# Attention into a gated MLP on one core: weight transfers a piece ahead, moves four a step, the low halves split later, output and spatial groups alternating

## The chip, the core and the metric

The kernel runs on one core of a Trainium2 chip. The metric is device microseconds of that core, lower is better: the median of three runs before the change is 774.14 us (772.09 to 775.22).

## The reference

Eight batches of 576 positions. Attention with 8 heads of 64, masked by blocks of 64 positions, is followed by a gated MLP whose gate mixes positions (`w_spatial`). All is float32.

```python
scores = q @ k.T / sqrt(64)                  # per batch and head, 576 x 576, block-causal mask
attn   = exp(scores - max) / (sum + 1e-9)
x      = attn @ v                            # heads side by side: 576 x 512 per batch
h      = max(x @ w_in, 0)                    # 512 -> 1024
u, v   = h[..., :512], h[..., 512:]
v_n    = (v - mean(v)) / sqrt(var(v) + 1e-6)
v_s    = einsum('ts,bsd->btd', w_spatial, v_n) + b_spatial
out    = (u * v_s) @ w_out                   # 512 -> 512
```

## The kernel before

The work is laid out by hand in **steps**, counted by `n`. Heads go in pairs, four pairs a batch, 32 pairs in all, and a pair takes `NS = 7` steps (`i` is the step within the pair, `g` the pair). In each step the program text issues, in a fixed order, a few instructions for each engine. `own` keeps every compute instruction in program order on its engine, so an instruction that waits holds back all that stands behind it on that engine. A step is an order and not a time: an engine runs on into later steps as far as its waits let it.

One pair passes through these stations:

- `load_pair` (SP, step 0 of the pair before): queries and keys into `raw`. `prep_pair`: ScalarE rounds them to `hi`, GpSimd subtracts for `lo` in four pieces (lines 237 to 251). Batch 0 uses `raw` directly, later batches three products of `hi` and `lo`.
- `scores_last` and `scores` (TensorE, steps 0 and 3; in batch 0 also 1 and 5): the last 64 queries of both heads first, then two banks at a time. `scores_last` needs the **last** of the four `lo` pieces in its third matmul.
- `exps` (VectorE maximum, ScalarE exponential; one slot a step), `norm` (VectorE reciprocal, GpSimd scaling, in the step after the slots 0, 2, 4 and 6).
- turning the probabilities: in batch 0 and for the last pair TensorE does it (`transposes_pe`, two steps after the slot) and ScalarE copies the result out at once, in batch 0 into the one tile `turned`. All other pairs turn 32x32 blocks on VectorE (`transposes`, three steps after), into a tile `q`, and `move` puts the quarters in place in `turned` with 16 transfers, all issued in step 3 of the next pair.
- `av` (TensorE): attention times values, at step `AV_AT = 17` after the pair's start, `BOOT_AV = 9` in batch 0, `LAST_AV = 10` for the last pair. ScalarE and VectorE split the result into the two halves of `x`.

When a batch's last `av` is out, `begin` puts the MLP's 29 **groups** of matmuls in `queue`: five `v_group`, eight `u_group`, and for each half `z` of the positions four `sp_group` (the spatial product, followed by gate and split into `gh` and `gl`) and four `out_group`. A credit counter lets them out at about one a step, at the end of the step, after the attention work. Each group's follow-up work is hung on later steps with `later(steps, phase, f)`: phase 0 opens a step, phase 1 follows exps, transposes and norm, phase 2 closes it.

The weights come in pieces (eight of `w_in`, four and a tail of `w_spatial`, four of `w_out`). `prep_w` issues one transfer into a staging buffer (the buffers of `gh` and `gl`, one each), four VectorE operations, one ScalarE copy and one GpSimd subtraction; `spread` hands these out over given steps as background work, emitted behind phase 1.

```python
        due(1)
        step_background(n)
        if at(n - 2) and by_pe(at(n - 2)[:2]):
            for j in TURNS[(i - 2) % NS]:
                transposes_pe(*at(n - 2)[:2], j)
        credit = min(credit + rate, 2.0)
        while credit >= 1.0 and queue and queue[0][0]():
            queue.pop(0)[1]()
            credit -= 1.0
```

## Time and profile before

| | before |
|---|---|
| median of 3 runs | 774.14 us |
| profiled run: time, span | 776.13 us, 774.3 us |
| granted TensorE clock, mean | 0.947 |
| busy: TensorE / VectorE / ScalarE / GpSimd | 695.3 / 468.5 / 430.8 / 341.5 us |
| first scores of batch 1 (step 28) | at 70.19 us |
| first MLP group of batch 0, of batch 1 | at 80.50, 204.76 us |
| first MLP group of the last batch | at 716.34 us |

Busy time says how long an engine had an instruction in work. TensorE is the engine with the most of it, so the first thing to look for is where TensorE sat idle, or ran at a lower granted clock, and what it waited for there.

### The profile page before, as it was taken

How to read it: one execution, taken by the hardware profiler on the slowest of the kernel's cores; microseconds unless marked ns; L12 is line 12 of the kernel's file. 1: busy time of each engine (PE TensorE's matmuls, PEld its weight loads, DVE VectorE, ACT ScalarE, POOL GpSimd, SP SyncE). 2: the span in 40 equal slices, each digit the busy share in tenths (PEclk: the TensorE clock that was granted, in tenths of full speed). 3: DMA queues.
4: the chain of work that ended last, by engine and by line, in shares of the span. 5: the costliest groups of instructions: out<-in, count | busy, mean ns of one | idle time of the engine just before them, and what ended most of it. 6: DMA issues, size and time to landing. Idle time of an engine off the chain costs nothing.

```text
span 774.3 us, 16381 instructions
## 1 busy us (share of the span) xinstructions
PE 695.3 (90%) x5729; PEld 611.9 (79%) x5729; DVE 468.5 (61%) x1587; ACT 430.8 (56%) x1156; POOL 341.5 (44%) x525
## 2 busy tenths in 40 slices
PE   6885943979998999899998999899998999899998
PEld 4554732968887988798887988798897988789897
DVE  5766837847666667665576666766676567521430
ACT  5665754545565547655575556755655556542542
POOL 3546644645433653355432663265435544231011
PEclk9797975999999999999998999999999999899999
DMA  6332253256554555546553565556553655140001
GB/s 212 105 105 93 81 141 115 67 127 174 156 125 96 148 150 149 133 114 157 147 133 76 144 156 132 133 152 162 149 121 89 174 154 122 39 124 25 15 13 49
DMA packets 42150, 92.05 MB, mean 119 GB/s; under 512 B 9298, under 2 KB 18002, under 8 KB 42068
## 3 DMA queue, kind: packets, MB, share of 16 engines
q1 hardware_dynamic: 32852, 81.56, 41.0%
q10 hardware_dynamic: 9216, 9.44, 3.5%
q8 instruction: 45, 0.74, 0.4%
q14 instruction: 37, 0.30, 0.1%
HBM read 38.18 MB, written 9.44 MB: 61 GB/s over the span
## 4 chain that ended last, share of the span: by engine, by line
PE 57%; DVE 15%; DMA 8%; ACT 6%; POOL 5%; SPq 5%; issue 4%; POOLq 0%; ACTq 0%; DVEq 0%
PE mv L514 10%; PE mo L667 10%; PE ms L632 9%; PE avh L466 6%; PE mu L608 5%; PE s L284 5%; SPq L420 4%; PE avl L466 3%; DMA turned<-q 3%; DVE q L405 3%; PE avh L483 2%; DVE p L319 2%; POOL p L353 2%; DMA raw<-qk 2%; PE s L296 1%
## 5 line engine op out<-in xcount | busy, mean ns | idle before, releaser
L353 POOL TENSOR_SCALAR p<-p,ssum 128x384 f32<-128x384 f32 (+4 forms) x288 | 162.7, 579 | 253.3 <-DVE ssum L349 135.3
L335 ACT ACTIVATE p<-p,nmax 128x384 f32<-128x384 f32 (+4 forms) x288 | 167.1, 581 | 110.8 <-DVE nmax L319 68.9
L319 DVE CUSTOM_DVE_ANT_0 p<-s,mask 128x128 f32<-128x128 f32 (+3 forms) x256 | 117.9, 480 | 26.7 <-PE s L284 26.5
L405 DVE STREAM_TRANSPOSE q<-p 128x384 f32<-128x384 f32 (+1 forms) x189 | 110.1, 615 | 9.7 <-DMA turned<-q 8.8
L608 PE MATMUL mu<-x,wi_hi 128*128 128x288 f32 x512 | 114.9, 306 | 0.0
L248 POOL TENSOR_TENSOR lo<-raw,hi 128x288 fp32r<-128x288 f32 x112 | 92.1, 848 | 1.0 <-ACT hi L244 1.0
L608 PEld LDWEIGHTS mu<-x,wi_hi 128*128 128x128 f32 x512 | 88.1, 196 | 3.1 <-issue 0.4
L651 POOL TENSOR_TENSOR gl<-u,gh 128x288 fp32r<-128x288 f32 x64 | 51.1, 806 | 88.4 <-ACT gh L650 88.4
L641 DVE TENSOR_TENSOR u<-ms,u 128x288 f32<-128x288 f32 x64 | 29.1, 454 | 92.7 <-PE ms L637 92.7
L514 PE MATMUL mv<-wi_hi,x 128*128 128x512 f32 x256 | 85.1, 395 | 0.0
L667 PE MATMUL mo<-gl,wo_hi 128*128 128x288 f32 x256 | 77.5, 303 | 3.8 <-POOL gl L651 3.3
L667 PE MATMUL mo<-gh,wo_hi 128*128 128x288 f32 x256 | 78.1, 305 | 0.0
L632 PE MATMUL ms<-ws_hi,vh 128*128 128x288 f32 x256 | 77.1, 301 | 0.3 <-DVE x L441 0.3
L667 PE MATMUL mo<-gh,wo_lo 128*128 128x288 f32 x256 | 75.5, 295 | 0.0
L632 PE MATMUL ms<-ws_hi,vl 128*128 128x288 f32 x256 | 75.4, 294 | 0.0
L632 PE MATMUL ms<-ws_lo,vh 128*128 128x288 f32 x256 | 75.3, 294 | 0.0
L608 PE MATMUL mu<-x,wi_lo 128*128 128x288 f32 x256 | 72.4, 304 | 0.0
L284 PE MATMUL s<-hi 64*128 64x128 f32 (+1 forms) x224 | 48.8, 388 | 17.1 <-DVE nmax L319 16.9
L466 PE MATMUL avh<-turned,v 128*64 128x128 f32 x868 | 57.0, 286 | 0.0
L514 PEld LDWEIGHTS mv<-wi_hi,x 128*128 128x128 f32 x256 | 48.1, 188 | 10.9 <-PE s L284 0.4
L667 PEld LDWEIGHTS mo<-gl,wo_hi 128*128 128x128 f32 x256 | 48.1, 188 | 8.1 <-POOL gl L651 7.5
L544 DVE BATCH_NORM_STATS2 st<-vr 128x6 f32<-128x512 f32 (+1 forms) x40 | 27.5, 689 | 44.4 <-ACT vr L532 44.0
(120 smaller groups left out, 1561.5 us busy)
## 6 DMA issues: line engine op xcount, KB each, us to landing
turned<-q SPq DMA_DIRECT2D x216, 100.0 KB, 3.5
turned<-q SPq DMA_DIRECT2D x216, 96.0 KB, 2.2
raw<-qk SPq DMA_DIRECT2D x31, 608.0 KB, 4.6
v<-v SPq DMA_DIRECT2D x32, 320.0 KB, 3.2
outT<-o ACTq DMA_DIRECT2D x64, 144.0 KB, 2.4
rwi<-w_in SPq DMA_DIRECT2D x8, 512.0 KB, 3.9
rwo<-w_out SPq DMA_DIRECT2D x4, 512.0 KB, 3.7
rws<-w_spT SPq DMA_DIRECT2D x4, 288.0 KB, 2.9
```

Source lines behind the costliest of these rows:

```text
L248: own(nc.gpsimd.tensor_tensor(out=lo[:, cs], in0=raw[:, cs], in1=hi[:, cs].bitcast(F32), op=ALU.subtract))
L284: own(nc.tensor.matmul(banks[(b, pr, i + hd)][:, o:o + n], a[js, qs], k[js, :n], start=(m == 0), stop=(m == len(parts) - 1),))
L319: own(nc.vector.tensor_tensor_reduce(out=pt[:, o:o + n], in0=bk[:, o:o + n], in1=mask[:, 512 - n:], scale=-0.125, scalar=BIG, op0=ALU.add, ...
L335: own(nc.scalar.activation(pt[:, o:o + n], pt[:, o:o + n], AF.Exp, bias=mx, scale=-1.0, accum_out=ssum[:, s0 + r:s0 + r + 1],))
L353: own(nc.gpsimd.tensor_scalar(out=pt[:, o:o + w], in0=pt[:, o:o + w], scalar1=ssum[:, r:r + 1], scalar2=1.0, op0=ALU.mult, op1=ALU.mult,))
L405: own(nc.vector.transpose(to[:, :, o:o + 32 * n].rearrange("p r (c j) -> p c r j", j=32), pt[:, :n * P].rearrange("p (c r j) -> p c r j", ...
L466: own(nc.tensor.matmul(out[js, (t0 - q0) * P:(t1 + 1 - q0) * P].rearrange("p (t a j) -> p a t j", a=4, j=32), vt[:, c, js], src[:, :, o:o ...
L514: own(nc.tensor.matmul(ps, xs[k][:, j, cs], w[:, k, DH:], start=(n == 0), stop=(n == 3 * NC - 1),))
L608: own(nc.tensor.matmul(ps[:, :HT], w[:, k, ds], xs[k][:, j, zs], start=(n == 0), stop=(n == 3 * NC - 1),))
L632: own(nc.tensor.matmul(ps[:, :HT], a[:, ds], w[:, k, zs], start=(n == 0), stop=False))
L651: own(nc.gpsimd.tensor_tensor(out=gl[:, dc, :], in0=uz, in1=gh[:, dc, :].bitcast(F32), op=ALU.subtract))
L667: own(nc.tensor.matmul(ps[:, :HT], w[:, k, es], a[:, k, :], start=(n == 0), stop=(n == 3 * ND - 1),))
```

## The change

- **Weights**: two staging buffers for each of the two tags; one generator, `ahead`, issues the transfer of the next piece before the work on the present one; the pieces are spread over other steps (1 to 53 instead of 2 to 45).
- **Moves**: `move` issues four transfers in each of the steps 3 to 6 instead of 16 in step 3.
- **Batch 0 and the last pair**: the turned probabilities get a `q` tile of their own (with its memset), the transposes come four steps after the slot instead of two, the copy out one step later still, and `av` at step 12 (before 9, and 10 for the last pair). `begin` of batch 0 comes at step 34 (before 30). The loads of the values move to later steps.
- **Splitting queries and keys**: `hi` and `lo` have one buffer instead of two. `prep_pair` runs in steps 4 and 5 of the pair before (two `lo` pieces in each) instead of 2 to 4.
- **Order in a step**: in steps 0 and 3 `exps` comes behind the transposes and `norm`. The last part of the normalisation of `v` moves to phase 2.
- **Groups**: the order starts `vv`; the output groups of half 0 alternate with the spatial groups of half 1; `gh` and `gl` have two buffers; the gate of the last spatial group of a half waits for the next step like the others.

```diff
-AV_AT, BOOT_AV, LAST_AV = 2 * NS + RUN2, NS + 2, NS + RUN2
+AV_AT, BOOT_AV = 2 * NS + RUN2, NS + 5
-    hl_p = ctx.enter_context(tc.tile_pool(name="hl_p", bufs=2))
+    hl_p = ctx.enter_context(tc.tile_pool(name="hl_p", bufs=1))
-        t = ff_p.tile([P, ND, HT], F32R, tag=tag, name=f"r{name}")
+        t = ff_p.tile([P, ND, HT], F32R, tag=tag, name=f"r{name}", bufs=2)
...
             own(nc.scalar.copy(hi[:, cs], raw[:, cs]))
         yield
-        yield
         for cs in (slice(S, S + HT), slice(0, HT), slice(HT, S), slice(S + HT, KQ)):
...
-        if (b, pr) == last and i == 0:
-            quarters[last] = tr_p.tile([P, 4, TW], F32, tag="q", name="q_last")
-            nc.gpsimd.memset(quarters[last][64:P, :, Q8O + P:], 0.0)
-        to = quarters.get((b, pr), turned)
+        if i == 0:
+            quarters[(b, pr)] = tr_p.tile([P, 4, TW], F32, tag="q", name=f"q_{b}_{pr}")
+            own(nc.gpsimd.memset(quarters[(b, pr)][64:P, :, Q8O + P:], 0.0))
+        to = quarters[(b, pr)]
...
+        later(1, 0, evac)
...
-    def move(b, pr):
+    def move(b, pr, a):
...
-            for a in range(4):
-                nc.sync.dma_start(turned[32 * r:32 * r + 32, a, :w], t[32 * a:32 * a + 32, r, :w])
+            nc.sync.dma_start(turned[32 * r:32 * r + 32, a, :w], t[32 * a:32 * a + 32, r, :w])
...
-            later(3, 1, rest)
+            later(3, 2, rest)
...
-            later(0 if dc == ND - 1 else 1, 2 if dc == ND - 1 else 0, gate)
-            later(0 if dc == ND - 1 else 1, 2 if dc == ND - 1 else 1, split_g)
+            later(1, 0, gate)
+            later(1, 1, split_g)
...
-        order = "vuvuvuvuvuuuu" if b else "v" * 5 + "u" * 8
+        order = "vvuvuvuvuuuuu" if b else "v" * 5 + "u" * 8
...
-        for z in range(2):
-            queue += sps[z] + outs[z]
-        return queue
+        queue += sps[0] + sps[1][:1]
+        for dc in range(1, ND):
+            queue += [outs[0][dc - 1], sps[1][dc]]
+        return queue + outs[0][ND - 1:] + outs[1]
...
+    def ahead(gens):
+        for k, g in enumerate(gens):
+            if k == 0:
+                next(g)
+            if k + 1 < len(gens):
+                next(gens[k + 1])
+            yield from g
...
+    spread(weights, 6 * NC, 1, U0 - 2)
+    spread(weights, 6 * NC, U0 - 2, U0 + 10)
+    spread(weights, 2 * FULL + 3, U0 + 10, U0 + 17)
+    spread(weights, 6 * ND, U0 + 17, U0 + 25)
+    spread(weights, None, U0 + 25, 0)
...
-            if i == 2 and b > 0:
-                spread(prep_pair(b, pr), 8, n, n + 4)
+            if i == RUN2 + 1 and b > 0:
+                spread(prep_pair(b, pr), 6, n, n + 2)
...
-                    later(1 if b else 0, 3, lambda b=b: begin(b))
-        if at(n - NS - RUN2) and i == RUN2 and not by_pe(at(n - NS - RUN2)[:2]):
-            move(*at(n - NS - RUN2)[:2])
-        if here:
+                    later(1, 3, lambda b=b: begin(b))
+        if g > 0 and RUN2 <= i < RUN2 + 4 and at(n - NS) and not by_pe(pairs[g - 1]):
+            move(*pairs[g - 1], i - RUN2)
+        runs = here and not boot and i in (0, RUN2)
+        if here and not runs:
             exps(*here, i)
...
+        if runs:
+            exps(*here, i)
...
-        if at(n - 2) and by_pe(at(n - 2)[:2]):
-            for j in TURNS[(i - 2) % NS]:
-                transposes_pe(*at(n - 2)[:2], j)
+        if at(n - 4) and by_pe(at(n - 4)[:2]):
+            for j in TURNS[(i - 4) % NS]:
+                transposes_pe(*at(n - 4)[:2], j)
```

## The prediction

> **What bounds the kernel now.** I read the page's busy line and slices first, then busy time by stage, then what TensorE waited for in each stage, and last the neighbours of the longest waits.

> ```profile
> PE 695.3 (90%) x5729; PEld 611.9 (79%) x5729; DVE 468.5 (61%) x1587; ACT 430.8 (56%) x1156; POOL 341.5 (44%) x525
> PE   6885943979998999899998999899998999899998
> PEclk9797975999999999999998999999999999899999
> 0.00:70.19 70.19, 51.51 (x352) 33.01 (x353) 46.33 (x147) 42.10 (x116) 35.31 (x57) 0.85 0.41 132
> 70.19:204.76 134.57, 100.51 (x831) 88.77 (x830) 84.51 (x277) 69.83 (x187) 71.09 (x98) 0.86 0.43 118
> 204.76:716.34 511.58, 489.06 (x4192) 439.25 (x4191) 321.18 (x1118) 296.42 (x804) 228.72 (x364) 0.98 0.50 128
> 462.98:546.32 83.34, 80.36 (x707) 72.28 (x706) 56.43 (x197) 50.84 (x140) 40.02 (x64) 1.00 0.54 139
> ```

> The stage rows give start and end, length, busy time of TensorE, its weight loads, VectorE, ScalarE and GpSimd, then the granted clock. TensorE bounds the kernel from 204.76 us on (489.06 of 511.58 us busy, clock 0.98). Before that it is idle for 204.76 - 51.51 - 100.51 = 52.7 us, at a clock of 0.85. So there are two questions: how much of the first 205 us comes back, and whether the dense part stays dense. Its last row is one batch's period (29 groups and 28 steps of attention) at full clock: 83.3 us.

> The largest hole is one wait of 19 us:

> ```profile
> 126.95 0.61 PE L296 MATMUL s<-hi,lo 128*128 128x288 f32 x1 [19.22 <-POOL lo L248]
> POOL ws_b L197 <- ACT ws_a L194: 7.1, 1, 7.1
> ACT ws_a L194 <- DMA rwt<-w_spT: 8.1, 1, 8.1
> DVE fwo L149 <- DMA rwo<-w_out: 14.2, 2, 11.1
> 100.68 10.13 SPq L420 DMA_DIRECT2D turned<-q  x16
> 110.85 0.59 SPq L190 DMA_DIRECT2D rwt<-w_spT  x1
> 112.35 11.48 SPq L141 DMA_DIRECT2D rwo<-w_out  x3
> SPq L257 <- PE avh L483: 28.0, 4, 9.7
> 126.95:139.50 12.55, 9.92 (x50) 9.23 (x51) 10.71 (x32) 4.87 (x15) 5.97 (x7) 0.58 0.32 96
> ```

> TensorE waits for `lo`; on GpSimd the rest of `lo` stands behind a weight subtraction, that waits for ScalarE, ScalarE for a weight transfer, and that one was queued on SP behind 16 moves that took 10.13 us. VectorE waited 11.1 us for the next piece. SP itself was held four times, 28.0 us, by a load of values that waited for `av`. After the hole TensorE ran 12.55 us at a clock of 0.58.

> **The change part by part.** First the 28 steps of batch 0.

> ```profile
> PE t L382 <- POOL p L353: 15.6, 11, 5.5
> L162 DVE SCALAR_TENSOR_TENSOR fwi<-rwi,fwi 128x512 int32<-128x512 int32 x7 | 5.9, 842 | 0.1
> L149 DVE TENSOR_SCALAR fwi<-rwi 128x512 f32<-128x512 f32 x7 | 4.6, 653 | 1.7 <-DMA rwi<-w_in 1.7
> L319 DVE CUSTOM_DVE_ANT_0 p<-s,mask 128x128 f32<-128x128 f32 (+3 forms) x256 | 117.9, 480 | 26.7 <-PE s L284 26.5
> L405 DVE STREAM_TRANSPOSE q<-p 128x384 f32<-128x384 f32 (+1 forms) x189 | 110.1, 615 | 9.7 <-DMA turned<-q 8.8
> 340.34 0.30 POOL L491 TENSOR_SCALAR xs<-x 128x128 fp32r<-128x128 f32 x1
> ```

> TensorE's transposes stand one step behind `norm` and wait 15.6 us for it. Four steps after the slot they stand three behind `norm`, and the copy out has a step of its own: these waits go. What is late next is ScalarE and VectorE, busy 42.10 and 46.33 of 70.19 us; the wait is worth between 0 (they are the bound) and 15.6 us. Both have room, and VectorE gets less weight work here (24 operations instead of some 47 up to step 28), so I take 10: step 28 at 60 us. Small prices inside that: the `q` memsets (four, GpSimd; nearest row the 0.30 us copy) are covered by GpSimd's 35 us of slack; the five `p` buffers are now held up to five steps, so that `exps` in an even step waits for the same step's transposes (0 to 0.5 us a time, taken as nothing, since TensorE runs ahead there).

> Steps 28 to 36 have no groups now (`begin` at 34 with a credit of 0.88 a step: the first group is out in step 36; before, in step 32). TensorE has attention alone, so VectorE sets the pace: the maxima take 117.9 / 32 and the transposes 110.1 / 27, together 7.8 us a pair, with some 2 us of small work (an estimate from the rows of its smaller groups) 1.4 us a step, 11 for eight steps. 16 background operations are 2.7 pieces of four VectorE operations at 0.75 us (between the two rows above), 8 us. Together 19 us: step 36 at 79 us.

> From step 36 to 68 come the 29 groups and 32 steps of attention. That is the steady period and four steps of attention more: 87 us at full clock (between 83.3 and 83.3 x 32 / 28 = 95, near the low end, since no groups are added). Weight transfers now lead by a piece, SP has four moves (10.13 / 4 = 2.5 us) between them instead of 16, and the loads of values come later in the order and hold SP less: the 19.22 us wait goes, and the slow clock behind it. Late next: VectorE with five `v_group` follow-ups in a row, and the `w_out` transfers, which in steps 45 to 49 stand behind moves that wait for `av`; for both I add 4 us, and 6 us for three waits on `lo` of the kind below. First group of batch 1: 79 + 87 + 10 = 176 us instead of 204.76. **First term: -28 us** (ends: -15 if the boot wait only moves and the weights stall VectorE again; -38 if neither costs anything).

> Dense part, what goes:

> ```profile
> PE s L284 <- DVE nmax L319: 11.1, 10, 1.9
> PE avl L466 <- DMA turned<-q: 2.5, 3, 1.8
> PE mo L667 <- POOL gl L651: 2.3, 7, 0.3
> 328.21 0.50 PE L284 MATMUL s<-hi 64*128 64x512 f32 x1 [1.90 <-DVE nmax L319]
> 328.20:331.40 3.20, 3.19 (x19) 2.12 (x21) 2.61 (x8) 3.20 (x11) 0.39 (x2) 0.56 0.01 3
> 370.91 0.44 PE L466 MATMUL avl<-turned,v 128*64 128x256 f32 x2 [1.76 <-DMA turned<-q]
> 370.90:374.00 3.10, 3.09 (x57) 2.95 (x58) 1.85 (x7) 0.44 (x2) 1.83 (x5) 1.00 0.41 138
> 667.29 0.48 PE L382 MATMUL t<-ident,p 128*128 128x128 f32 x1 [3.83 <-POOL p L353]
> 670.00:673.00 3.00, 3.00 (x17) 2.62 (x17) 0.09 (x1) 0.92 (x3) 0.00 (x0) 0.50 0.00 0
> ```

> Once a batch (five times) the scores wait 2.2 us for a bank that VectorE frees late, because the last `v_group`'s follow-up is in its way; 3.2 us at a clock of 0.56 follow, 1.4 us more. The order `vv` brings that follow-up a step earlier, `rest` goes behind `exps`: 5 x 3.6 = 18 us. The waits for `turned` and `gl` go with the alternation (4 us of 4.8). In the last batch the transposes' 3.83 us wait and the half clock behind it (two stretches, 5.7 us) go: 3.8 + 2.8 = 7 us. That is **-22 and -7**. The moves split over steps cost and bring nothing here: SP has only loads between them, and waits for data, not for steps.

> Dense part, what comes. `prep_pair` now issues its last two `lo` pieces in step 5 **behind** `norm` of slots 3 and 4 (and behind phase 1's `gl`), where before all four stood in steps 3 and 4, ahead of it. The next `scores_last` needs the last piece. Where that `norm` stands is in the trace:

> ```profile
> 317.96 0.29 PE L296 MATMUL s<-hi 128*128 128x288 f32 x1
> 317.40 1.14 POOL L353 TENSOR_SCALAR p<-p,ssum 128x384 f32<-128x384 f32 x2
> 341.11 0.29 PE L296 MATMUL s<-hi 128*128 128x288 f32 x1
> 341.37 0.29 PE L296 MATMUL s<-hi,lo 128*128 128x288 f32 x1
> 338.67 1.71 POOL L248 TENSOR_TENSOR lo<-raw,hi 128x288 fp32r<-128x288 f32 x2
> 340.77 1.15 POOL L353 TENSOR_SCALAR p<-p,ssum 128x384 f32<-128x384 f32 x2
> 341.88 0.81 POOL L651 TENSOR_TENSOR gl<-u,gh 128x288 fp32r<-128x288 f32 x1
> 359.68 0.30 PE L296 MATMUL s<-hi 128*128 128x288 f32 x1
> 358.56 1.15 POOL L353 TENSOR_SCALAR p<-p,ssum 128x384 f32<-128x384 f32 x2 [2.88 <-DVE ssum L349]
> ```

> `scores_last` needs the last piece in its third matmul, 0.27 us after its first (341.11, 341.37). That `norm` starts 0.56, 0.34 and 1.12 us before the next scores in three of a batch's four pairs (`u`, spatial and spatial groups around it; in the fourth, with two `v_group` ahead of the scores, there is room). It cannot start earlier in the new order: VectorE gets to it through work that waits for the previous step's group. With 1.15 for `norm` and 1.71 for two pieces, `lo` is complete 2.3, 2.5 and 1.7 us after the scores want to start, and 0.8 later in the second case (`gl`): waits of 2.0, 3.0 and 1.4 us. By the code's credit count such pairs come 6, 5 and 5 times: 12 + 15 + 7 = 34 us. Does the clock drop behind them? A wait of 1.90 us (with 0.33 just before) was followed by 0.56, one of 1.76 by 1.00. So the five long ones and half of the first kind pay 1.4 us: 8 x 1.4 = 11. **Together +45** (ends: 0 if GpSimd is in time after all; 16 x (3.0 + 1.4) = 70 if each is like the dearest).

> [...]

> The single `hi`/`lo` buffer itself costs nothing: the copies of step 4 overwrite what the scores of step 3 have read, and ScalarE gets there after its own `exps` of that step. `exps` behind `norm` in steps 0 and 3 shifts VectorE's 1.4 us of other work ahead of it; the banks it frees are wanted three steps later.

> Sum: -28 - 22 - 7 + 45 = -12 us against the profiled run's 776.1 (span 774.3 and 1.8 around it): 764. That run stands 2 us above the median of 774.14, so the predicted median is **762 us**.

> **The rivals.**

> *No new wait.* GpSimd reaches the last `lo` pieces in time, because VectorE comes to `norm` earlier when gates and transposes no longer hold it. For it: GpSimd is busy only 228.72 of 511.58 us, and in the fourth pair kind there is room. Against: `norm` starts as late as it does by VectorE's order, which step 5 keeps. Without the 45, and with half of the bank waits left (no pause ahead of them): 774.1 - 28 - 7 - 11 = 728 us.

> *Slower: the `lo` wait costs more than all the rest.* One mechanism: in each of the 16 pairs `hi` is also cast later (step 4), so that the first two pieces push `norm` back as well. At 3.0 us and 1.4 us of clock each the waits take 70: 774.1 - 57 + 70 = 787. It decides from 57 / 16 = 3.6 us a pair on, clock included. For it: in the second kind `lo` already ended (338.67 + 1.71) just 0.39 us ahead of `norm`. Against: where 1.76 us was waited, no clock was lost.

> *The transfers still come late.* The change does not do what it says: weight pieces stand on SP behind moves that wait for `av`, VectorE stalls on `w_out` again, and the first term is -8: 774.1 - 8 - 29 + 45 = 782. Against: one piece of lead is two or more steps.

> **How the numbers follow.** Forecast 0.46 (own range 752 to 775), no new wait 0.20, slower 0.24, late transfers 0.10. The measurement tells 0.5% (3.9 us) from no change. Faster: most of the forecast (0.39) and the first rival: 0.59. Within 0.5%: the upper edge of the forecast and the lower edges of the last two: 0.12. Slower: the rest, 0.29. The range reaches into both sides: 733 to 789.

> **What would show it.** Right: the first `v_group` of batch 1 near 176 us; no wait above 5 us on `lo` in the first batch; in the dense part scores waiting for `lo` 1.4 to 3 us in three of four pairs, and no waits for the bank. Wrong: no rows of `s` released by `lo` after 200 us (then near 728), or the first term below 15 us, or a clock under 0.95 in the dense part.

## The result: 2.9% slower, and the profile after

The changed kernel takes 798.19 us (median of 4 runs, 791.4 to 799.82), the kernel before, run beside it, 774.68 us (4 runs, 772.09 to 775.87). The ratio is 1.029 [1.023, 1.036]. The forecast was 762, in a range that ended at 789: it had the wrong sign.

The profiled execution took 797.51 us, with a span of 795.7 (before 774.3). From its page, the busy line, the granted clock in 40 slices, the shares of the chain that ended last, and the group of the scores' third matmul with the idle time before it:

```profile
PE 715.7 (90%) x5729; PEld 635.5 (80%) x5729; DVE 465.2 (58%) x1587; ACT 426.4 (54%) x1156; POOL 342.6 (43%) x529
PEclk9997877989998999999998999999989889899999
PE 66%; POOL 13%; DVE 9%; issue 5%; ACT 4%; DMA 2%; SPq 1%; POOLq 0%; DVEq 0%; ACTq 0%
L295 PE MATMUL s<-hi,lo 128*128 128x288 f32 x56 | 22.3, 399 | 59.4 <-POOL lo L247 59.4
```

TensorE does the same 5729 matmuls and is busy for 20 us more. The work is the same, and the mean granted clock has fallen from 0.947 to 0.935, so I read the 20 us as clock. On the chain, SP's queue has fallen from 5% to 1% (the 19 us hole is gone) and GpSimd has risen from 5% to 13%. One group says nearly all of it: 59.4 us of idle time, all released by `lo`.

Busy time by stage, after (start and end, length, busy time of TensorE, weight loads, VectorE, ScalarE, GpSimd, then the granted clock), cut at the first `v_group` of batch 1 and of the last batch as in the prediction:

```profile
0.00:197.61 197.61, 160.62 (x1180) 129.22 (x1181) 128.75 (x430) 110.87 (x305) 108.76 (x157) 0.89 0.44 129
197.61:739.02 541.41, 501.49 (x4192) 455.44 (x4190) 320.00 (x1112) 293.25 (x802) 227.37 (x364) 0.95 0.44 120
739.02:795.70 56.68, 53.55 (x362) 50.80 (x360) 16.46 (x45) 22.31 (x51) 6.47 (x8) 0.99 0.08 26
```

| stage | before | after | difference | predicted |
|---|---|---|---|---|
| to the first `v_group` of batch 1 | 204.76 | 197.61 | -7.2 | -28 |
| dense part | 511.58 | 541.41 | +29.8 | +16 |
| of it idle TensorE | 22.5 | 39.9 | +17.4 | +15 |
| of it busy TensorE (clock) | 489.06 | 501.49 | +12.4 | +1 |
| rest | 58.0 | 56.7 | -1.3 | 0 |

(Predicted idle: -18.8 for the waits that go, +34 for those that come; predicted clock: -7 and -2.8 where half clock goes, +11 where it comes.) What TensorE waited for, after, in the dense part (us in total, times, longest):

```profile
PE s L295 <- POOL lo L247: 39.6, 18, 2.6
PE ms L630 <- ACT q L386: 0.2, 1, 0.2
```

and in the first batch:

```profile
PE s L295 <- POOL lo L247: 21.9, 8, 4.8
PE s L283 <- DVE nmax L318: 5.2, 9, 2.0
PE avl L464 <- DMA turned<-q: 2.2, 1, 2.2
```

In the dense part the waits of before are gone, the 11.1 us on the bank, the 3.83 on `norm` and the small ones (one of 0.2 us on ScalarE apart). In their place stands one that is new, on `lo`. Sixteen of the 18 are 2.3 to 2.6 us long. One of them, in the timeline of after, with ScalarE's cast of `hi`, GpSimd and TensorE:

```profile
332.48 1.31 ACT L244 CAST hi<-raw 128x576 fp32r<-128x576 f32 x2
333.92 1.57 POOL L247 TENSOR_TENSOR lo<-raw,hi 128x288 fp32r<-128x288 f32 x2 [4.30 <-issue]
335.88 1.15 POOL L352 TENSOR_SCALAR p<-p,ssum 128x384 f32<-128x384 f32 x2
337.00 0.79 POOL L649 TENSOR_TENSOR gl<-u,gh 128x288 fp32r<-128x288 f32 x1
337.75 1.68 POOL L247 TENSOR_TENSOR lo<-raw,hi 128x288 fp32r<-128x288 f32 x2
336.73 0.29 PE L295 MATMUL s<-hi 128*128 128x288 f32 x1
336.86 0.29 PE L295 MATMUL s<-lo,hi 128*128 128x288 f32 x1
339.48 0.40 PE L295 MATMUL s<-hi,lo 128*128 128x288 f32 x1 [2.32 <-POOL lo L247]
```

`hi` is cast by 333.8. GpSimd does two pieces at 333.92, then `norm` (1.15 us), then `gl` (0.79), and only at 337.75 the two pieces that the scores want at about 337.1. The two pieces that stand ahead of `norm` are done by 335.5; the other two would have been by 337.2, had they stood beside them. This is the prediction's arithmetic, down to the `gl`.

### The profile page after: what moved, and what is told of

Its sections match the earlier page's. It is cut to its first block, busy times and chain, and to the rows that moved or that the text cites. A ratio compares the mean times of both kernels' runs of the same rounds, so it can differ in the third digit from the quotient of the medians.

```text
span 795.7 us, 16364 instructions
## 1 busy us (share of the span) xinstructions
PE 715.7 (90%) x5729; PEld 635.5 (80%) x5729; DVE 465.2 (58%) x1587; ACT 426.4 (54%) x1156; POOL 342.6 (43%) x529
## 3 DMA queue, kind: packets, MB, share of 16 engines
q1 hardware_dynamic: 32852, 81.56, 37.8%
## 4 chain that ended last, share of the span: by engine, by line
PE 66%; POOL 13%; DVE 9%; issue 5%; ACT 4%; DMA 2%; SPq 1%; POOLq 0%; DVEq 0%; ACTq 0%
PE mo L664 10%; PE ms L630 10%; PE mu L606 10%; PE s L283 9%; PE mv L512 9%; POOL lo L247 7%; PE avh L464 6%; POOL p L352 4%; PE s L295 3%; PE avl L464 3%; DVE p L318 2%; PE avh L481 2%; DVE q L408 2%; ACT p L334 1%; PE t L380 1%
## 5 line engine op out<-in xcount | busy, mean ns | idle before, releaser
L247 POOL TENSOR_TENSOR lo<-raw,hi 128x288 fp32r<-128x288 f32 x112 | 95.3, 872 | 110.4 <-issue 89.0
L606 PE MATMUL mu<-x,wi_hi 128*128 128x288 f32 x512 | 119.9, 316 | 0.0
L606 PEld LDWEIGHTS mu<-x,wi_hi 128*128 128x128 f32 x512 | 91.9, 204 | 3.7 <-issue 0.9
L630 PE MATMUL ms<-ws_hi,vh 128*128 128x288 f32 x256 | 82.7, 323 | 0.2 <-ACT q L386 0.2
L630 PE MATMUL ms<-ws_lo,vh 128*128 128x288 f32 x256 | 79.6, 311 | 0.0
L630 PE MATMUL ms<-ws_hi,vl 128*128 128x288 f32 x256 | 79.6, 311 | 0.0
L295 PE MATMUL s<-hi,lo 128*128 128x288 f32 x56 | 22.3, 399 | 59.4 <-POOL lo L247 59.4
L295 PEld LDWEIGHTS s<-hi,lo 128*128 128x128 f32 x56 | 12.7, 227 | 64.5 <-POOL lo L247 64.5
L512 PEld LDWEIGHTS mv<-wi_hi,x 128*128 128x128 f32 x256 | 48.4, 189 | 10.8 <-issue 0.6
L630 PEld LDWEIGHTS ms<-ws_hi,vh 128*128 128x128 f32 x256 | 52.4, 205 | 3.0 <-issue 1.3
L334 ACT ACTIVATION_READ_ACCUMULATOR p<-p,nmax 128x1 f32 x288 | 54.3, 189 | 0.0
```

Of the source, the lines that this page charges most:

```text
L247: own(nc.gpsimd.tensor_tensor(out=lo[:, cs], in0=raw[:, cs], in1=hi[:, cs].bitcast(F32), op=ALU.subtract))
L295: own(nc.tensor.matmul(bk[z][:, :HT], a[:, Q8:], k[:, z * HT:(z + 1) * HT], start=(m == 0), stop=(m == len(parts) - 1),))
L334: own(nc.scalar.activation(pt[:, o:o + n], pt[:, o:o + n], AF.Exp, bias=mx, scale=-1.0, accum_out=ssum[:, s0 + r:s0 + r + 1],))
L512: own(nc.tensor.matmul(ps, xs[k][:, j, cs], w[:, k, DH:], start=(n == 0), stop=(n == 3 * NC - 1),))
L606: own(nc.tensor.matmul(ps[:, :HT], w[:, k, ds], xs[k][:, j, zs], start=(n == 0), stop=(n == 3 * NC - 1),))
L630: own(nc.tensor.matmul(ps[:, :HT], a[:, ds], w[:, k, zs], start=(n == 0), stop=False))
```

## The experiments

Each kernel ran beside the kernel before on the same chip; kernels grouped by letter shared a chip. Ratios are to the kernel before, with 95% intervals. Comparisons between letters go across chips, on which the kernel before took 773.4 to 775.2 us. The stages come from one profiled run of each kernel.

| run | edit | us | ratio |
|---|---|---|---|
| after | | 798.19 | 1.029 [1.023, 1.036] |
| e1 | after, split of queries and keys a step earlier | 751.96 | 0.969 [0.964, 0.974] |
| e3 | after, all four `lo` pieces in step 4 | 750.63 | 0.968 [0.965, 0.971] |
| e2 | before, with the split as in after | 844.09 | 1.087 [1.080, 1.093] |
| g6 | before, with the split as in e1 | 780.50 | 1.009 [1.006, 1.012] |
| f1 | e1, `exps` first in all steps | 743.00 | 0.958 [0.953, 0.964] |
| f2 | e1, all group order as before | 741.88 | 0.959 [0.955, 0.962] |
| g5 | f2 and f1 together | 741.63 | 0.957 [0.951, 0.964] |
| g2 | e1, only `vv` undone | **725.26** | **0.935 [0.930, 0.940]** |
| h1 | g2, `u` first | 766.32 | 0.988 [0.982, 0.993] |
| f3 | e1, 16 moves in one step | 745.56 | 0.965 [0.959, 0.970] |
| f4 | e1, weights without lead | 753.61 | 0.974 [0.971, 0.977] |
| g1 | f4 and f3 together | 754.87 | 0.973 [0.968, 0.979] |

The theory after the result: the place of two `lo` pieces behind `norm` costs more than the whole change brings. Its rivals: the single `hi`/`lo` buffer, the waits on the bank that would appear without them, or a clock that other things pull down.

### Where the pieces stand: e1, e3, e2, g6

**e1** moves the split one step ahead, so that all pieces stand in front of the `norm` of slots 3 and 4; everything else of the change stays.

```diff
-            if i == RUN2 + 1 and b > 0:
+            if i == RUN2 and b > 0:
                 spread(prep_pair(b, pr), 6, n, n + 2)
```

> The changed kernel with one edit: the split of the next pair's queries and keys starts in step 3 of the pair before instead of step 4, so that its last two lo pieces stand ahead of norm of slots 3 and 4 on GpSimd, not behind it. Theory (the late lo is the whole loss): the waits of the scores for lo (61.5 us in all, 16 of 2.3 to 2.6 us in the dense part) go almost wholly, and the half clock behind them, 16 x 1.4 = 22 us in the dense part; some 5 to 10 us of bank waits come back: about 725 us, between 715 and 745. Rival (the alternating groups and the new order of exps make VectorE and GpSimd late, and lo is only where it shows): the waits move to another releaser and the time stays above 765 us.

Measured: 751.96 us, 46 less than the change and 23 less than before. e1's dense stage, in the columns of the stage view:

```profile
184.22:687.86 503.64, 488.48 (x4192) 442.55 (x4191) 322.71 (x1114) 294.94 (x800) 224.31 (x362) 0.97 0.48 130
```

The longest entry of what TensorE waited for in that stage of e1:

```profile
PE s L283 <- DVE nmax L318: 14.2, 11, 2.0
```

And GpSimd's `lo` of one pair, from e1's timeline:

```profile
286.99 3.25 POOL L247 TENSOR_TENSOR lo<-raw,hi 128x288 fp32r<-128x288 f32 x4 [0.74 <-ACT hi L244]
```

All four pieces run in one go, and no wait on `lo` is left in the dense part. It is 37.8 us shorter than in after: 24.8 of idle time and 13.0 of busy time, that is of clock. The first batch gets 13.4 us back (184.22 against 197.61). So the place of the split costs 46 us; this edit moves the cast of `hi` as well, and e3 tells the two apart. The 752 us lie above the 715 to 745 expected, since more waits on the bank came back than the 5 to 10 us allowed for. And the waits on the bank are there again, 14.2 us against 11.1 before: in after they had only been hidden behind the longer wait.

**e3** leaves the split where the change put it, and issues the four pieces in one step.

```diff
-                spread(prep_pair(b, pr), 6, n, n + 2)
+                spread(prep_pair(b, pr), 6, n, n + 1)
```

> The changed kernel with all four lo pieces issued in step 4 (still behind the cast of hi in step 4, but ahead of norm of slots 3 and 4 in step 5). Theory (what hurts is standing behind norm and the gate's gl): lo is complete 1.15 us (norm) and in one pair kind 0.8 us (gl) earlier, and no longer waits for VectorE's reciprocal: waits of 0 to 0.7 us are left, about 735 us, between 725 and 755. Rival (the cast of hi in step 4 is what is too late): waits of 1.5 us and more stay, above 770 us.

Measured: 750.63 us, the same as e1. What TensorE waited for over e3's whole span:

```profile
PE s L295 <- POOL lo L247: 18.8, 19, 1.7
PE s L283 <- DVE nmax L318: 17.6, 17, 2.0
```

The waits on `lo` shrink from 61.5 to 18.8 us without the split moving: what matters is that no `norm` stands between the pieces. The 1 us a time that is left fits the cast of `hi`, which is still a step later than in e1: in e3 GpSimd stands idle ahead of `lo` until that cast has ended, 107.5 us in 27 times (20.3 us in e1).

**e2** puts the late split, with its single buffer, into the kernel before, and nothing else.

```diff
-    hl_p = ctx.enter_context(tc.tile_pool(name="hl_p", bufs=2))
+    hl_p = ctx.enter_context(tc.tile_pool(name="hl_p", bufs=1))
...
-        yield
...
-            if i == 2 and b > 0:
-                spread(prep_pair(b, pr), 8, n, n + 4)
+            if i == RUN2 + 1 and b > 0:
+                spread(prep_pair(b, pr), 6, n, n + 2)
```

> The kernel before with this part of the change alone: one hi/lo buffer, and the split in steps 4 and 5 of the pair before, two lo pieces behind norm. Theory (the late lo is enough by itself, whatever the group order): 16 or more waits of 2 to 2.6 us in the dense part plus 1.4 us of clock each, less 18 us of bank waits that go, and about 10 us in the first batch: +50 us, about 820 us, between 800 and 840. Rival (it needs the new group order): three waits a batch of under 1 us, below 790 us.

Measured: 844.09 us, 69 more than before and a little above the 800 to 840 expected. What TensorE waited for in e2:

```profile
PE s L295 <- POOL lo L247: 68.5, 31, 3.4
PE s L295 <- ACT hi L244: 17.6, 1, 17.6
```

Its dense stage:

```profile
219.91:789.14 569.23, 510.89 (x4191) 458.88 (x4190) 323.01 (x1114) 298.96 (x802) 228.27 (x364) 0.94 0.42 115
```

The late split makes the kernel before slower by more than it does the changed one, so no other part of the change is needed for the loss. This edit has two things in it, the place and the single buffer, and **g6** keeps the buffer and takes the place back:

```diff
-            if i == RUN2 + 1 and b > 0:
+            if i == RUN2 and b > 0:
                 spread(prep_pair(b, pr), 6, n, n + 2)
```

> The kernel before with one hi/lo buffer, and the split begun in step 3 of the pair before (two lo pieces in step 3, two in step 4). Theory (neither the single buffer nor one step costs anything; only standing behind norm did): within 5 us of the kernel before, 770 to 780, against 844 of e2_before_late_lo. Rival (the single buffer ties the split to the end of the scores, and costs by itself): 785 us and more.

Measured: 780.5 us, 1.009 [1.006, 1.012] of before. Of e2's 69 us the place is 64. About 6 are left for the single buffer, together with the cast of `hi`, which is a step later than before. g6's dense stage is that of before (512.10 us, TensorE busy 489.07 of it). Its first batch is 2.5 us longer in the profiled run (207.29 us against 204.76), with waits of 10.2 us on `hi` and 9.2 on `lo`; where the rest of the 6 lies was not taken apart.

### The order of the groups: f1, f2, g5, g2, h1

With the pieces mended, which part of the new order brings the rest? e1 has `exps` behind `norm` in two steps, the order `vv`, and the alternation of output and spatial groups. **f1** undoes the first, **f2** the other two with the gate, **g5** all three.

```diff
-        runs = here and not boot and i in (0, RUN2)
+        runs = False
```

> The changed kernel with the split of queries and keys from step 3 (as in e1_lo_step3, 752 us) and with exps ahead of transposes and norm in every step, as before. Theory (exps behind norm is what frees the banks late): the bank wait of 2.4 us a batch that e1 still shows, and the slow clock behind it, go: 735 to 745 us. Rival (the bank wait is VectorE's follow-up of the v groups, as it was before the change, with exps first): the wait stays near 2.2 us, time within 4 us of 752.

```diff
-            later(1, 0, gate)
-            later(1, 1, split_g)
+            later(0 if dc == ND - 1 else 1, 2 if dc == ND - 1 else 0, gate)
+            later(0 if dc == ND - 1 else 1, 2 if dc == ND - 1 else 1, split_g)
...
-        order = "vvuvuvuvuuuuu" if b else "v" * 5 + "u" * 8
+        order = "vuvuvuvuvuuuu" if b else "v" * 5 + "u" * 8
...
-        queue += sps[0] + sps[1][:1]
-        for dc in range(1, ND):
-            queue += [outs[0][dc - 1], sps[1][dc]]
-        return queue + outs[0][ND - 1:] + outs[1]
+        for z in range(2):
+            queue += sps[z] + outs[z]
+        return queue
```

> e1_lo_step3 with the order of the groups as before the change: v and u in turn, spatial and output groups of a half one after the other, the last gate of a half in the same step. Theory (the alternation hides nothing, since TensorE waited only 0.33 us a batch for gl): within 4 us of 752. Rival (the alternation is worth what the dense part gained, 511.6 - 503.6 = 8 us): about 760 us.

> f2_groups_as_before (741.9 us) with exps first in every step, too, as f1 (743.0). Theory (both act on the same bank wait, so they do not add; exps first with v and u in turn is the order of the kernel before, which waited 2.2 us a batch): 742 to 752 us. Rival (two gains that add): 732 to 737.

Measured: 743.0, 741.88 and 741.63 us. Each undoing alone makes e1 faster by about 1%, and both together bring no more than one: they do not add. For f1 that 1% stands at the edge of the noise (its interval and e1's just fail to overlap). In f1 the bank wait is still 1.9 us a batch: the time fell into the range of its theory, but the wait that the theory would remove is there. In f2 it is 0.97, and waits on `gl` appear (5.9 us, 10 times) that the alternation had removed.

**g2** undoes only `vv` and keeps the alternation and the late `exps`.

```diff
-        order = "vvuvuvuvuuuuu" if b else "v" * 5 + "u" * 8
+        order = "vuvuvuvuvuuuu" if b else "v" * 5 + "u" * 8
```

> e1_lo_step3 with one line of the group order as before (v and u in turn in place of vv first), the alternation of output and spatial groups kept. Theory (vv first is what costs: the bank wait is 0.97 us a batch in f2 against 2.4 in e1): about 743 us, between 739 and 747. Rival (the alternation is what f2 gained by undoing): within 4 us of 752.

Measured: 725.26 us, the fastest of all, 49.5 us under the kernel before; no theory had its size. So `vv` cost 27 us (e1 against g2), and the alternation with the later gate is worth 17 (f2 against g2). In the profiled runs 10 us of the second difference lie ahead of batch 1 (191.18 against 180.98 us) and 8 in the dense part; f2's 5.9 us on `gl` are a third of it, and the rest was not taken apart. g2's dense stage:

```profile
180.98:663.50 482.52, 474.82 (x4192) 430.88 (x4191) 323.45 (x1114) 293.33 (x800) 227.65 (x362) 1.00 0.50 136
```

Its largest wait of TensorE there:

```profile
PE s L283 <- DVE nmax L318: 5.8, 6, 1.0
```

VectorE around the first `exps` of a pair, between the pair's first scores and the scores of step 3, which wait for a bank, from the timeline of e1:

```profile
293.95 0.29 PE L295 MATMUL s<-hi 128*128 128x288 f32 x1
295.80 0.69 DVE L582 TENSOR_TENSOR vl<-vr,vh 128x512 fp32r<-128x512 f32 x1 [0.93 <-ACT vh L574]
297.59 0.69 DVE L542 BATCH_NORM_STATS2 st<-vr 64x6 f32<-64x512 f32 x1
299.78 0.44 DVE L327 CUSTOM_DVE_ANT_0 p<-s,mask 128x288 f32<-128x288 f32 x1
304.19 0.42 DVE L318 CUSTOM_DVE_ANT_0 p<-s,mask 128x256 f32<-128x256 f32 x1
304.67 0.50 PE L283 MATMUL s<-hi 64*128 64x512 f32 x1 [2.01 <-DVE nmax L318]
```

The same place in the timeline of g2:

```profile
206.61 0.29 PE L295 MATMUL s<-hi 128*128 128x288 f32 x1
209.07 0.44 DVE L327 CUSTOM_DVE_ANT_0 p<-s,mask 128x288 f32<-128x288 f32 x1
210.11 1.12 DVE L582 TENSOR_TENSOR vl<-vr,vh 128x512 fp32r<-128x512 f32 x1
212.31 0.69 DVE L542 BATCH_NORM_STATS2 st<-vr 64x6 f32<-64x512 f32 x1
215.45 0.50 PE L283 MATMUL s<-hi 64*128 64x512 f32 x1 [0.96 <-DVE nmax L318]
```

In e1 the follow-ups of a `v_group` stand ahead of the pair's first `exps`, whose maximum starts 5.8 us after the pair's first scores. The bank that the scores of step 3 want is freed two slots later, by the maximum at 304.19, and they wait 2.01 us. In g2 the first maximum starts 2.5 us after the first scores, the same work runs behind it, and the wait is 0.96. The dense stage's clock goes from 0.97 to 1.00, and with it 13.7 us of TensorE's busy time; idle time falls by 7.5.

**h1** goes one letter further and starts with a `u` group, which moves the `v` groups by one place again.

```diff
-        order = "vuvuvuvuvuuuu" if b else "v" * 5 + "u" * 8
+        order = "uvuvuvuvuvuuu" if b else "v" * 5 + "u" * 8
```

> g2_v_u_in_turn (725.3 us) with the groups starting u, so that each v group comes one place later still. Theory (what counts is which exps the follow-up of the last two v groups stands ahead of on VectorE: in e1 it stands ahead of the first of the next pair, in g2 behind that one; here it falls ahead of the third, and the scores of step 3 wait for that one's bank): a bank wait of 1.5 us or more a batch, 728 to 740 us. Rival (later is simply better): 722 us or less, with bank waits under 0.96 us.

Measured: 766.32 us, 41 above g2; the direction and the place of the wait were expected, not the size. VectorE and TensorE in h1:

```profile
225.56 0.68 DVE L536 TENSOR_TENSOR vr<-mv,vr 64x512 f32<-64x512 f32 x1
226.73 0.69 DVE L542 BATCH_NORM_STATS2 st<-vr 64x6 f32<-64x512 f32 x1
227.94 0.41 DVE L318 CUSTOM_DVE_ANT_0 p<-s,mask 128x256 f32<-128x256 f32 x1
228.41 0.79 PE L283 MATMUL s<-hi 64*128 64x512 f32 x1 [4.03 <-DVE nmax L318]
```

The follow-ups now stand right in front of the maximum that frees the bank (at 227.94), as the theory had it, and the wait is 4.03 us. Three orders of the same groups give 752, 725 and 766 us, in the order of their bank waits, 2.01, 0.96 and 4.03.

### Transfers: f3, f4, g1

Before, a 19 us hole came from weight transfers queued behind 16 moves. Was it the lead of a piece, the split of the moves, or the later handover that closed it?

```diff
-        if g > 0 and RUN2 <= i < RUN2 + 4 and at(n - NS) and not by_pe(pairs[g - 1]):
-            move(*pairs[g - 1], i - RUN2)
+        if g > 0 and i == RUN2 and at(n - NS) and not by_pe(pairs[g - 1]):
+            for a in range(4):
+                move(*pairs[g - 1], a)
```

> e1_lo_step3 with all 16 moves issued in step 3, as before. Theory (with a piece of lead the weights bear 10 us of moves on the queue): within 4 us of 752. Rival (the moves on the queue were the cause of the 19 us hole of the kernel before): a wait of 5 us or more in the first batch, 760 to 772 us.

f4 takes away `ahead` and puts the weights back at their old steps, with `w_out` five steps later, as the groups are:

```diff
-    weights = ahead(
...
+    spread(chain([prep_w_in(c, 1) for c in range(NC)]), 7 * NC + 1, 2, 18)
+    spread(chain([prep_w_in(c, 0) for c in range(NC)]), 7 * NC + 1, 18, U0 + 5)
+    spread(chain([prep_w_sp(c) for c in range(FULL)] + [prep_w_tail()]), 3 * FULL + 5, U0 + 5, U0 + 12)
+    spread(chain([prep_w_out(c) for c in range(ND)]), 7 * ND + 1, U0 + 15, U0 + 22)
```

> e1_lo_step3 with the weights as before: no transfer ahead, the steps of before (w_out five steps later, since the first groups also come later). Theory (the lead and the new steps give most of the 20 us that the first batch gained): 765 to 775 us, with VectorE and ScalarE waiting for weight transfers again. Rival (the first batch gained by its own tiles, later transposes and later handover): within 5 us of 752.

g1 has both edits.

> e1_lo_step3 with both transfer parts undone: no lead and old steps for the weights (as f4, 753.6 us), and 16 moves in step 3 (as f3, 745.6). Theory (either part alone keeps the weights from standing behind the moves, so the hole of 19 us in the kernel before needs both undone): a wait of 10 us or more in the first batch comes back, 765 to 775 us. Rival (the hole left with the later handover of batch 0, and the transfers are not the cause any more): within 4 us of f4, 750 to 757.

Measured: 745.56, 753.61 and 754.87 us, against e1's 751.96; the intervals of all three overlap e1's. The first `v_group` of batch 1 comes at 180.93, 189.98 and 190.79 us, e1's at 184.22. Splitting the moves brings nothing, and the queue shows why. This is SP in after, where four moves a step were meant:

```profile
87.43 10.12 SPq L422 DMA_DIRECT2D turned<-q  x16
```

The 16 moves run in one block all the same, since nothing else stands between them on SP. The lead may be worth some 6 us in the first batch of the profiled run. The whole time does not show it clear of noise, and the first group of batch 0 alone comes at 78.8 to 82.6 us in e1, f2, f3 and g2, which are the same up to there. Neither part brings the hole back: g1's longest wait on `lo` is 3.6 us. In g6, which keeps the old handover and the old loads, waits of 10 us stand in the first batch. What closed the hole is therefore among the parts that g1 still shares with the change, that is, the turned tiles of batch 0, the later handover, the second staging buffers, the later loads of values and of the last weights; which of these was not tried.

## Why the prediction was wrong

The forecast was -12 and the measured difference of the spans +21.4 us. The miss of 33.4 is 20.8 in the first term, 13.8 in the dense part, -1.3 in the rest.

**First term, -28, measured -7.2: the step that failed most.** Step 28 came at 56.8 us (60 said): the boot waits did go. The first group came 26.1 us later instead of 19, at 82.9 (79 said). From the first group to batch 1 it took 114.7 us instead of 97:

```profile
82.88:197.61 114.73, 97.10 (x718) 86.15 (x717) 77.05 (x239) 59.92 (x162) 61.30 (x80) 0.86 0.46 123
```

Those 97 were 87 at full clock and 10 for waits. TensorE was idle for 17.6 and busy for 97.1 at a mean clock of 0.86, so most of this miss is clock: the prediction had let the slow clock go with the 19 us hole. It had counted 6 us of waits on `lo` for the batch, "three waits of the kind below"; there were 21.9 us in eight, 8.7 of them ahead of the first group and 13.1 behind it. One of the two dearest, on GpSimd and TensorE in after, shows why they are longer than those below:

```profile
100.25 1.14 POOL L352 TENSOR_SCALAR p<-p,ssum 128x384 f32<-128x384 f32 x2
101.36 1.83 POOL L128 TENSOR_TENSOR ws_lo<-rws,ws_hi 128x576 fp32r<-128x576 f32 x1
103.16 1.68 POOL L247 TENSOR_TENSOR lo<-raw,hi 128x288 fp32r<-128x288 f32 x2
104.89 0.40 PE L295 MATMUL s<-hi,lo 128*128 128x288 f32 x1 [4.16 <-POOL lo L247]
```

In the first batch GpSimd also subtracts weights, and that 1.83 us stands between `norm` and `lo` too. The longest wait, 4.84 us, has the same form. The prediction had counted the weight work as a load on VectorE and did not put it into GpSimd's order. Nor did the four moves a step that it counted on reach SP's queue. e1 gives 13.4 of the 20.8 back, about half of it idle time and half clock. Of the other 7 the runs show only that VectorE holds TensorE there (e1: 10.8 us of waits on maxima from the first group to batch 1); it was not taken apart. The rival with late transfers had named a first term of -8, but its mechanism did not come: VectorE has no wait on `w_out` in after.

**The waits that come, 34 us: right.** Sixteen waits, as counted, of 2.39, 2.32 and 2.63 us in place of 2.0, 3.0 and 1.4: 39.2 us. The count and the kind were right; the three sizes were off by up to 1.2 us, and that the sum comes so near owes something to luck. The rival that ended slower had them dearer still, with the first pieces pushing `norm` back. They did not: in the quoted pair they end 0.4 us before it. Its 787 us lies nearest to the 798 measured, but not by its mechanism.

**Their clock, 11 us for half of them: too low.** The clock over the 6.5 us behind seven of the sixteen waits, from the stage view of after:

```profile
226.56:233.06 6.50, 6.50 (x41) 6.20 (x42) 5.23 (x22) 3.72 (x9) 2.11 (x3) 0.74 0.54 170
249.01:255.51 6.50, 6.50 (x31) 6.00 (x32) 0.99 (x4) 1.19 (x3) 2.83 (x4) 0.50 0.59 178
273.61:280.11 6.50, 6.50 (x52) 6.20 (x53) 3.68 (x17) 2.48 (x8) 3.33 (x5) 1.00 0.62 196
318.35:324.85 6.50, 6.50 (x52) 6.15 (x52) 5.23 (x22) 3.72 (x9) 2.11 (x3) 1.00 0.51 164
339.48:345.98 6.50, 6.50 (x41) 6.16 (x42) 2.19 (x11) 1.67 (x6) 2.84 (x4) 0.74 0.69 205
590.00:596.50 6.50, 6.50 (x32) 6.00 (x33) 5.23 (x22) 3.72 (x9) 2.10 (x3) 0.51 0.50 160
638.63:645.13 6.50, 6.50 (x32) 6.00 (x33) 1.02 (x5) 0.87 (x2) 2.03 (x3) 0.53 0.70 205
```

Of all sixteen, five were followed by 1.00, five by 0.74 and six by 0.50 to 0.53. The missing clock adds up to 5 x 0.26 x 6.5 + 2.95 x 6.5 = 27.6 us, 1.7 a wait. Counted the same way, e1's six waits of about 2 us miss 12.5; the 15.1 between them come near the 13.0 of busy time that the dense parts differ by. So 11 of 16 waits paid, each of them more than the 1.4 that the prediction took from one stretch of 3.2 us, which was too short a look. In place of 11 us the clock behind the waits cost 27.6. In the table it is the row of busy time, +12.4 against +1, and so 11 of the 13.8 us that the dense part is off by.

**What goes in the dense part, -22: the 18 for the bank did not go by the step named.** The prediction said that `vv` brings the last `v_group`'s follow-up a step earlier. Counted by the code's credit, the fourth `v_group` leaves in the same step of the batch before and after. TensorE's timelines agree: the last `v_group`, a `u_group` and the next pair's scores start at 314.5, 316.4 and 318.0 us before, and at 290.5, 292.4 and 293.9 in e1. In g2 the last `v_group` (285.4) is followed by the scores at once (287.3): there its follow-up comes one place later, not earlier. e1 still waits 14.2 us for the bank, and undoing `vv` makes it 27 us faster. In after those waits vanished only because the pause for `lo` came first. The alternation was taken as 4 us and is worth 17 once `vv` is gone.

**At nothing.** The split of the moves (f3) brings nothing, as said. The single buffer costs 0.9% in the kernel before (g6, with the later cast), and in the dense part nothing, as said. `exps` behind `norm` was taken as free: it costs about 1% beside `vv` (e1 against f1), and nothing that can be told without `vv` and the alternation (f2 against g5). With the alternation and without `vv`, that is, g2 with `exps` first, it was not run.

Of the signs on the list, those of being right came in part (waits of 1.4 to 3 us on `lo` in three of four pairs, none above 5 us in the first batch, none for the bank in the dense part). So did one of being wrong (a first term below 15 us); the dense clock, 0.95, lies at the edge of another. The forecast knew the wait, and took its clock and the gains beside it from places that had not been counted as closely.

## What to carry to other kernels

In after's dense part GpSimd was busy for 227.37 of 541.41 us, and still TensorE waited 39.6 us there for its `lo`, since two pieces stood behind a `norm` that itself waits for VectorE (132.5 us in that stage). So do not count on slack: place what the bottleneck wants next ahead of work that waits for another engine, and read the place in the row list, with every other instruction that shares the queue in that stage. The sixteen waits of 2.3 to 2.6 us cost 1.7 us of clock each in the mean, and five of them none, so price a short wait of the bottleneck from several such waits. Test each part of a large change with the others undone one at a time: here two parts of the order hid a 50 us gain, one worth 46 us and one 27.

## What the runs showed of the hardware

Behind the waits of after the granted clock stood at 1.00 or at 0.50, and waits of like length had different outcomes: those of 2.32 to 2.40 us were followed by none, one or two stretches of 3.41 us at 0.50. TensorE was busy without a break before and after them (the waits that end at 226.56, 249.01 and 318.35, one of each outcome: 1.60 of 1.60 us ahead of the wait, 6.50 of 6.50 behind it). The stretches behind the first two waits, 3.42 and 6.83 us long:

```profile
228.34:231.76 3.42, 3.42 (x15) 3.42 (x16) 2.98 (x17) 1.92 (x4) 1.36 (x2) 0.50 0.61 229
248.82:255.65 6.83, 6.64 (x32) 6.14 (x33) 1.04 (x5) 1.19 (x3) 3.02 (x5) 0.50 0.57 171
```

Of e1's waits of 2.0 us one was followed by 1.00 and another by 0.53 over 6.5 us; all six of 4.0 us in h1 lost clock (0.51 to 0.75). With waits under 1 us in every batch but for a single one of 1.6 (g2) the dense clock was 1.00.
